# Attention and a four-expert layer on one core: the first batch runs two chunks alone, and the second batch's attention is traced inside them

## The chip, the core and the metric

The kernel runs on one core of a Trainium2 chip. TensorE (PE) multiplies matrices, VectorE (DVE), ScalarE (ACT) and GpSimd (POOL) do element-wise work, SyncE (SP) issues the DMAs. The metric is device time in microseconds (us), and lower is better. The profiled execution of the kernel before took 1321.44 us.

## The reference

Attention with a packed set of 32 queries in the middle, and then a mixture of four experts:

```python
def sm_attn(qq, kk, vv):
    s = scale * np.matmul(qq, kk.transpose(0, 1, 3, 2))
    s = s - np.max(s, axis=-1, keepdims=True)
    a = np.exp(s)
    a = a / (np.sum(a, axis=-1, keepdims=True) + 1e-09)
    return np.matmul(a, vv)
p_packed = sm_attn(p, k, v)                  # 8 batches, 8 heads, 32 packed queries, 576 keys
out = sm_attn(q, p_packed, p_packed)         # 576 tokens against the 32 packed rows
...
x = out.transpose(0, 2, 1, 3).reshape(B * S, H * D)          # 4608 x 512
p = domain_probs / (domain_probs.sum(-1, keepdims=True) + 1e-09)
for e in range(E):                           # 4 experts, 512 -> 1024 -> 512
    h = np.maximum(x @ w1[e], 0.0)
    out += p[:, e:e + 1] * (h @ w2[e])
```

All data are float32.

## The kernel before

**Units.** The expert layer is cut into 8 chunks of 512 hidden columns (`ch`, half an expert each) and the 8 batches into 4 pairs (`sb`). A unit is one chunk of one batch, and `units` lists the 64 of them in the order in which they run: chunk 0 for batch 0, chunk 0 for batch 1, chunk 1 for batch 0, and so on; after 16 units the next pair. The loop at L537 runs over them. Units are counted from 0 here.

**A unit's work.** `mm1_group` (four groups (kh, c), 12 matmuls each) multiplies the batch's token weights `xh`, `xl` (a value split into a rounded part and its rest) by `ghl`, and DVE (L310) applies relu and the probability `pbt`; the four blocks are `ablk`. `s_operand` forms with DVE (L327) the sums of a seven-product 2x2 block multiplication (`ORDER`), and splits each of the seven operands: ACT writes the rounded part (`hi_of`, L103), POOL the rest (`lo_of`, L108), both in `st`. `product` (seven per unit, 12 matmuls each) multiplies `st` by `tt`, the split block of w2, and ACT (chunk 0) or DVE (later chunks, L392) adds it to `acc`. During a unit's products the four mm1 groups of the next unit are issued between them (`GROUPS`), so PE does 84 + 48 matmuls of 288 columns per unit.

**What a unit needs beforehand.** `g_form(bs, ch, raws)` multiplies the packed attention rows `ppbd` of the batches `bs` by the w1 chunk `raws` (`wraw`) and gives `ghl`; the main loop calls it for both batches of a pair at once. `t_form(ch)` loads the w2 blocks of a chunk and makes its seven `tt` (DVE and POOL differences at L364, then the split); `tt` has 8 buffers. `t_store` writes each `tt` to `td` in DRAM while pair 0 runs, and `t_load` reads it back when a chunk comes again.

**Attention.** `pack_unit(bs, g)` (g is one half of the heads) loads k and v, multiplies p by k (`scores`), takes the softmax, transposes it (`tr`), multiplies it by v (L195) and leaves `ppbd`. `tok_unit(bs, g)` loads q, multiplies it by `ppbd`, takes the softmax over 32 rows (DVE L226, L231, L236, L242; ACT L233; DVE or POOL L232, L239) and leaves `xh`, `xl`. Both are generators, cut into steps at each `yield`; `wavefront` and `drain` run the steps. Tiles of the pool `att` (`att_tile`) have two buffers for `kt` (k or q) and `a1`, and one for `vt` (v) and `at`. For the pairs after the first, `AT_FIRST` and `AT_LATER` say at which unit a generator begins.

**The start.** Before the loop (L485 to L517) the kernel runs the attention of batches 0 and 1, `g_form` of chunk 0 for each, `t_form(0)` and the four mm1 groups of unit 0. This part is called the preparation below.

**Order.** TensorE's order within `together` is fixed by hand; the rest of each engine's order is set by a scheduler that goes through the traced program with its own estimate of times. Each engine then runs its list in order, and so does SP with the DMAs: a waiting instruction holds up everything behind it on its engine.

## Time and profile before

| | before |
|---|---|
| runs | 1322.88, 1323.24, 1323.43 us (median 1323.24) |
| profiled execution | 1321.44 us, of which the span of its instructions is 1319.6 us |
| PE / DVE / POOL / ACT busy | 1271.7 / 966.4 / 859.4 / 475.0 us |
| mean granted clock of TensorE | 0.987 of 2.4 GHz |
| DMA | 209 MB, 158 GB/s on the mean |

Times in the rows are counted from the first instruction. A row of the timeline gives its start, its length, the engine, the line of the kernel, the tile written and the tiles read (out<-in), the shapes and the number of instructions merged in it; in brackets stands how long the engine was idle before it, and who ended that wait. PE, PEld are matmuls and weight loads; a trailing q (SPq) marks the queue that issues DMAs. Matmuls overlap, so their rate is read from the distance of starts, not from their length. A matmul at L74 is recorded twice in the counts (x32 for the 16 matmuls of `scores` on both halves).

### The profile page before, as it was taken

To read this page: it belongs to the slowest core of one execution; us is meant where nothing else is said; L and a number is where in the kernel's file an instruction comes from. 1 tells how busy PE (TensorE), PEld (TensorE's weight loads), DVE (VectorE), ACT (ScalarE), POOL (GpSimd) and SP (SyncE) were. 2 spreads that over 40 slices of the span, in tenths; PEclk is the share of its full clock that TensorE was granted. 3 is DMA by queue.
4 is the path that set the end of the run, shared out by engine and by line. 5 is a ranking of instruction groups with operands and counts; after the bars stand their busy time and mean duration, and the time that the engine had idled before them with its cause. 6 is when DMAs were issued, how large, how long until landed. Compare 5 with 4: busy or idle time off the path is not lost.

```text
span 1319.6 us, 26648 instructions
## 1 busy us (share of the span) xinstructions
PE 1271.7 (96%) x10720; PEld 1178.2 (89%) x10720; DVE 966.4 (73%) x1334; ACT 475.0 (36%) x784; POOL 859.4 (65%) x578
## 2 busy tenths in 40 slices
PE   4799999899999999999999999999999999999997
PEld 2698989798899999999999998999999999999997
DVE  5767778989895676888687566699669466666668
ACT  3454434343334333333334433233323533323231
POOL 5678778798986454557568454566558655555556
PEclk8999999999999999999999999999999999999998
DMA  9536464445354545554335645443446443334422
GB/s 350 185 117 225 162 213 150 153 170 188 137 198 154 167 146 184 174 180 130 119 108 201 205 157 174 133 138 121 154 138 203 152 138 116 119 126 153 128 96 73
DMA packets 86811, 208.99 MB, mean 158 GB/s; under 512 B 8736, under 2 KB 31392, under 8 KB 86688
## 3 DMA queue, kind: packets, MB, share of 16 engines
q1 hardware_dynamic: 86016, 207.13, 46.8%
q8 instruction: 86, 1.41, 0.4%
q14 instruction: 37, 0.30, 0.1%
q10 hardware_dynamic: 672, 0.15, 0.1%
HBM read 168.37 MB, written 38.87 MB: 157 GB/s over the span
## 4 chain that ended last, share of the span: by engine, by line
PE 78%; DVE 12%; POOL 6%; DMA 2%; issue 1%; ACT 0%; POOLq 0%; SPq 0%; DVEq 0%; ACTq 0%
PE dbl L66 73%; PE dbl L74 4%; DVE sblk L327 3%; POOL st L108 3%; DVE ablk L310 1%; DVE acc L392 1%; POOL tt L108 1%; POOL acc L442 1%; PE dbl L69 1%; DVE ghl L108 1%; DVE acc L442 1%; DMA pnd<-pb 1%; DVE a L226 0%; DVE a L232 0%; DVE nb L167 0%
## 5 line engine op out<-in xcount | busy, mean ns | idle before, releaser
L66 PEld LDWEIGHTS dbl<-st,tt 128*128 128x128 f32 x5376 | 731.8, 189 | 67.7 <-POOL st L108 33.8
L66 PE MATMUL dbl<-st,tt 128*128 128x288 f32 x5376 | 774.8, 298 | 11.4 <-POOL st L108 5.2
L108 POOL TENSOR_TENSOR st<-sblk,st 128x576 fp32r<-128x576 f32 x256 | 395.4, 1551 | 215.4 <-ACT st L103 212.9
L66 PE MATMUL dbl<-xh,ghl 128*128 128x288 f32 x2048 | 418.4, 296 | 1.8 <-DVE ghl L108 1.8
L108 POOL TENSOR_TENSOR st<-ablk,st 128x576 fp32r<-128x576 f32 x192 | 286.8, 1497 | 186.5 <-ACT st L103 178.3
L392 DVE TENSOR_TENSOR acc<-dbl,acc 128x576 f32<-128x576 f32 x385 | 288.8, 752 | 118.9 <-PE dbl L66 116.5
L66 PEld LDWEIGHTS dbl<-xh,ghl 128*128 128x128 f32 x2048 | 331.0, 189 | 2.7 <-DVE ghl L108 2.7
L66 PE MATMUL dbl<-xl,ghl 128*128 128x288 f32 x1024 | 304.5, 297 | 11.5 <-POOL xl L108 5.2
L310 DVE SCALAR_TENSOR_TENSOR ablk<-dbl,pbt 128x576 f32<-128x576 f32 x256 | 192.5, 752 | 160.2 <-PE dbl L66 155.6
L103 ACT CAST st<-sblk 128x576 fp32r<-128x576 f32 x256 | 172.9, 676 | 302.2 <-DVE sblk L327 210.4
L103 ACT CAST st<-ablk 128x576 fp32r<-128x576 f32 x192 | 129.7, 676 | 227.2 <-PE dbl L66 216.3
L66 PEld LDWEIGHTS dbl<-xl,ghl 128*128 128x128 f32 x1024 | 193.6, 189 | 13.9 <-POOL xl L108 5.7
L103 ACT CAST ghl<-dbl 128x512 fp32r<-128x512 f32 x128 | 75.0, 586 | 150.9 <-PE dbl L74 89.7
L327 DVE TENSOR_TENSOR sblk<-ablk 128x576 f32<-128x576 f32 x128 | 120.3, 940 | 9.8 <-POOL acc L442 0.5
L108 DVE TENSOR_TENSOR ghl<-dbl,ghl 128x512 fp32r<-128x512 f32 x128 | 87.5, 684 | 11.3 <-ACT ghl L103 7.9
L327 DVE TENSOR_TENSOR sblk<-ablk,sblk 128x576 f32<-128x576 f32 x64 | 69.0, 1078 | 6.8 <-POOL st L108 0.9
L74 PE MATMUL dbl<-wraw,ppbd 64*32 64x512 f32 x1024 | 71.8, 602 | 0.3 <-ACT acc L390 0.3
L108 POOL TENSOR_TENSOR tt<-b,tt 128x512 fp32r<-128x512 f32 x42 | 59.5, 1427 | 4.1 <-ACT tt L103 4.0
L442 POOL TENSOR_TENSOR acc<-acc,acc 128x576 f32<-128x576 f32 x28 | 47.3, 1700 | 20.1 <-DVE acc L392 20.1
L327 DVE TENSOR_TENSOR sblk<-sblk,ablk 128x576 f32<-128x576 f32 x64 | 57.6, 899 | 1.6
L390 ACT COPY acc<-dbl 128x576 f32<-128x576 f32 x56 | 35.6, 641 | 39.7 <-PE dbl L66 39.6
L103 ACT CAST tt<-b 128x512 fp32r<-128x512 f32 x42 | 25.0, 619 | 35.5 <-DVE b L364 14.3
(63 smaller groups left out, 434.1 us busy)
## 6 DMA issues: line engine op xcount, KB each, us to landing
tt<-td SPq DMA_DIRECT2D x168, 512.0 KB, 4.3
wraw<-in_w SPq DMA_DIRECT2D x128, 256.0 KB, 3.1
td<-tt SPq DMA_DIRECT2D x56, 512.0 KB, 3.4
kt<-in_k SPq DMA_DIRECT2D x16, 576.0 KB, 6.0
kt<-in_q SPq DMA_DIRECT2D x16, 576.0 KB, 6.0
pbt<-pnd SPq DMA_DIRECT2D x32, 288.0 KB, 4.3
out<-acc SPq DMA_DIRECT2D x32, 288.0 KB, 2.4
vt<-in_v SPq DMA_DIRECT2D x16, 512.0 KB, 6.4
```

The source lines that it names most:

```text
L66: on_pe(nc.tensor.matmul(**kw))
L69: on_pe(nc.tensor.transpose(**kw))
L74: ins = nc.tensor.matmul(**kw).ins
L103: nc.scalar.copy(out=dst, in_=src)
L108: eng.tensor_tensor(out=dst, in0=src, in1=hi.bitcast(F32), op=ALU.subtract)
L310: nc.vector.scalar_tensor_tensor(out=a, in0=ps[:, :, 0:HS], scalar=0.0, in1=pbt[b][:, ts].rearrange("p (o t) -> p o t", o=1).broadcast_to( ...
L327: nc.vector.tensor_tensor(out=t, in0=blk(x), in1=blk(y), op=op)
L390: nc.scalar.copy(out=accs[b, i], in_=psv)
L392: nc.vector.tensor_tensor(out=accs[b, i], in0=psv, in1=accs[b, i], op=ALU.add)
L442: eng.tensor_tensor(out=m[dst], in0=m[x], in1=m[y], op=op)
```

## The change

`units[1]` and `units[2]` change places: batch 0 runs chunk 0 and chunk 1 (units 0 and 1), then batch 1 runs chunk 0 and chunk 1 (units 2 and 3); from unit 4 on the list is as before. The preparation holds batch 0 alone. Its q is loaded right after k and v, ahead of w1, and w1 ahead of w2. The attention of batch 1 is the generator `second`, whose steps are traced between the products of units 0 and 1 by the table `SECOND` (the 20 at unit 1 is never needed in full: `drain(second)` stands before it); its tiles all come from `att`. `g_form` for chunk 1 is called for each batch by itself, w1 of chunk 0 is loaded a second time, `t_form(1)` runs in unit 0, and `tt` of chunks 0 and 1 is read back from `td` during units 1 and 2. The attention of batches 2 and 3 begins at units 4, 7, 9 and 12 instead of 2, 5, 8 and 11.

```diff
@@ -280,6 +280,7 @@
             yield
 
     units = [(sb, ch, 2 * sb + i) for sb in range(SB) for ch in range(NCH) for i in range(2)]
+    units[1], units[2] = units[2], units[1]
     pbt = {}
 
     def load_probs(b, e):
@@ -470,51 +471,39 @@
 
     hpool = ctx.enter_context(tc.tile_pool(name="hpool", bufs=1, reuse_waits="tile"))
     with ExitStack() as first:
-        pools = [first.enter_context(tc.tile_pool(name=f"unit{u}", bufs=1)) for u in range(3)]
+        pools = [first.enter_context(tc.tile_pool(name=f"unit{u}", bufs=1)) for u in range(NG)]
 
         def unit_tile(u):
-            def new(b, shape, name):
-                if u == 3 or u == 2 and name in ("kt", "a1"):
-                    return att_tile(b, shape, name)
-                return pools[u].tile(shape, F32, name=name)
-            return new
+            return lambda b, shape, name: pools[u].tile(shape, F32, name=name)
 
         def form_tile(shape, name):
             return hpool.tile(shape, F32, name="st", bufs=4) if name == "b2" else hpool.tile(shape, F32, name="ablk", bufs=6)
 
-        packs = [pack_unit([b], g, unit_tile(2 * b + g)) for b in range(2) for g in range(NG)]
-        toks = [
-            tok_unit([b], g, unit_tile(2 * b + g), nc.gpsimd if g else nc.vector, nc.gpsimd if b else nc.scalar)
-            for b in range(2) for g in range(NG)
-        ]
+        def tok_tile(g):
+            return lambda b, shape, name: att_tile(b, shape, name) if name != "at" or g else pools[0].tile(shape, F32, name=name)
+
+        packs = [pack_unit([0], g, unit_tile(g)) for g in range(NG)]
+        toks = [tok_unit([0], g, tok_tile(g), nc.gpsimd if g else nc.vector) for g in range(NG)]
         forms = t_form(0, form_tile, {n: nc.gpsimd for n in ("t1", "t2", "t3", "t4")})
         norm_probs()
         for i in (0, 1, 0, 1):
             next(packs[i])
-        next(forms)
-        raws = w1_load(0)
-        drain(wavefront(packs[:2], 1))
         for i in range(2):
             next(toks[i])
-        for i in (2, 3, 2, 3):
-            next(packs[i])
+        raws = w1_load(0)
+        next(forms)
+        load_probs(0, 0)
+        drain(wavefront(packs, 1))
         for i in range(2):
             next(toks[i])
-        for b in range(2):
-            load_probs(b, 0)
         for _ in range(3):
             next(forms)
         drain(g_form([0], 0, raws))
-        drain(wavefront(toks[:2], 1))
+        drain(wavefront(toks, 1))
         drain(forms)
-        drain(wavefront(packs[2:], 1))
-        for i in range(2, 4):
-            next(toks[i])
         for kh, c in ((0, 0), (0, 1), (1, 1), (1, 0)):
             mm1_group(0, kh, c)
-        drain(g_form([1], 0, raws))
         raws = w1_load(1)
-        drain(wavefront(toks[2:], 1))
 
     apool = ctx.enter_context(tc.tile_pool(name="apool", bufs=2, reuse_waits="tile"))
     rpool = ctx.enter_context(tc.tile_pool(name="rpool", bufs=1, reuse_waits="tile"))
@@ -528,8 +517,14 @@
 
     nothing = iter(())
     GROUPS = {1: ((0, 0),), 3: ((0, 1),), 4: ((1, 1),), 6: ((1, 0),)}
-    GROUPS_FIRST = {4: ((0, 0), (0, 1)), 5: ((1, 1),), 6: ((1, 0),)}
-    AT_FIRST = ((2, pack_unit, 0), (5, pack_unit, 1), (8, tok_unit, 0), (11, tok_unit, 1))
+    GROUPS_LATE = {4: ((0, 0), (0, 1)), 5: ((1, 1),), 6: ((1, 0),)}
+    AT_FIRST = ((4, pack_unit, 0), (7, pack_unit, 1), (9, tok_unit, 0), (12, tok_unit, 1))
+
+    second = chain(
+        wavefront([pack_unit([1], g, att_tile) for g in range(NG)], 1),
+        wavefront([tok_unit([1], g, att_tile, nc.gpsimd if g else nc.vector) for g in range(NG)], 1),
+    )
+    SECOND = {0: (3, 3, 2, 2, 2, 2, 2), 1: (2, 2, 2, 20)}
 
     FORM_ODD, FORM_EVEN = (0, 2, 3, 5), (0, 1, 3)
     AT_LATER = ((1, pack_unit, 0), (4, pack_unit, 1), (7, tok_unit, 0), (9, tok_unit, 1))
@@ -548,9 +543,15 @@
 
         gsteps = nothing
         nsb, nch = (sb, ch + 1) if ch + 1 < NCH else (sb + 1, 0)
-        if not odd and nsb < SB:
+        if u == 0:
+            gsteps = g_form([0], 1, raws)
+        elif u == 2 or u == 3:
+            gsteps = g_form([1] if u == 2 else [0, 1], u - 1, raws)
+            drain(gsteps)
+            raws = w1_load(u)
+        elif u > 3 and not odd and nsb < SB:
             gsteps = g_form([2 * nsb, 2 * nsb + 1], nch, raws)
-        forming = odd and sb == 0 and ch + 1 < NCH
+        forming = u == 0 or u > 2 and odd and sb == 0 and ch + 1 < NCH
         if forming:
             tsteps = t_form(ch + 1, raw_tile, {"t1": nc.gpsimd, "t2": nc.vector, "t3": nc.vector, "t4": nc.gpsimd})
             next(tsteps)
@@ -562,26 +563,37 @@
             elif nxt:
                 s_operand(u + 1, n - NPROD)
             if nxt:
-                for grp in (GROUPS if u else GROUPS_FIRST).get(i, ()):
+                for grp in (GROUPS_LATE if u == 1 else GROUPS).get(i, ()):
                     mm1_group(u + 1, *grp)
-            if i in (3, 6):
+            if u == 0:
+                drain(gsteps)
+            elif i in (3, 6):
                 next(gsteps, None)
-            if i == 4 and u + 2 < len(units) and units[u + 2][1] % 2 == 0:
+            if u == 1 and i == 3:
+                drain(second)
+                drain(g_form([1], 0, raws))
+                raws = w1_load(1)
+            for _ in range(SECOND[u][i] if u in SECOND and i < len(SECOND[u]) else 0):
+                next(second, None)
+            if i == 4 and u > 1 and u + 2 < len(units) and units[u + 2][1] % 2 == 0:
                 load_probs(units[u + 2][2], units[u + 2][1] // 2)
             if i % 2 == 0:
                 next(back, None)
-            if sb == 0 and i in (FORM_ODD if odd else FORM_EVEN):
+            if sb == 0 and i in (FORM_ODD if odd or u == 0 else FORM_EVEN):
                 next(tsteps, None)
             next(sums, None)
             if sb == 0 and not odd:
                 t_store(ch, i)
-            if odd and nxt and not forming:
+            if nxt and not forming and (odd or u == 1):
                 t_load(nxt[1], i)
         drain(gsteps)
         drain(sums)
         if ch == NCH - 1 and b < B - 1:
             sums = combine(b)
-        if not odd:
+        if u == 0:
+            raws = w1_load(0)
+            load_probs(1, 0)
+        elif not odd and u > 2:
             nsb, nch = (sb, ch + 2) if ch + 2 < NCH else (sb + 1, ch + 2 - NCH)
             if nsb < SB:
                 raws = w1_load(nch)
```

The lists of the engines move as follows. Numbers tell buffers apart.

**The preparation, ACT and POOL.** ACT's list before, from the second w2 block to the first exponential of `tok_unit` (L233, on a1_331), where `tt` is being split (L103, the w2 blocks stand in ablk and st):

```order
L103 CAST tt_355<-ablk_184 128x512
L103 CAST tt_358<-ablk_182 128x512
L103 CAST tt_404<-ablk_182 128x512
L233 ACTIVATE a1_331<-a1_331 128x576
L103 CAST ghl_366<-dbl_361 128x512
```

The same place now (the exponential is that on a1_318):

```order
L188 COPY at_246<-dbl_247 128x512
L189 COPY at_246<-dbl_247 64x128
L103 CAST tt_333<-ablk_193 128x512
L103 CAST tt_338<-ablk_195 128x512
L103 CAST tt_341<-ablk_193 128x512
L233 ACTIVATE a1_318<-a1_318 128x576
L103 CAST ghl_349<-dbl_344 128x512
```

The exponential stands behind three splits of w2 blocks instead of four, and all three are of loads that now come after q and w1. POOL's list now, from the first half of the heads of batch 0 (xl_180<-at_378) to the first operands of unit 0 (st):

```order
L108 TENSOR_TENSOR xl_180<-at_378,xh_179 128x576
L239 TENSOR_TENSOR a1_330<-a1_330,s2_373 128x576
L365 TENSOR_TENSOR ablk_193<-ablk_193,st_197 128x512
L108 TENSOR_TENSOR xl_180<-at_382,xh_179 128x576
L108 TENSOR_TENSOR tt_391<-ablk_193,tt_391 128x512
L108 TENSOR_TENSOR tt_394<-st_197,tt_394 128x512
L108 TENSOR_TENSOR tt_397<-st_197,tt_397 128x512
L108 TENSOR_TENSOR tt_535<-b11_484,tt_535 128x512
L108 TENSOR_TENSOR st_476<-ablk_413,st_476 128x576
L108 TENSOR_TENSOR st_481<-sblk_479,st_481 128x576
```

Before, all seven `tt` of chunk 0 stood ahead of the first xl, and st followed the second xl at once; now four `tt` stand between the second xl and the first st.

**Unit 0, SP and PE.** SP's list now, around the load of v for the second half of the heads of batch 1 (vt_574):

```order
L219 DMA kt_805<-in_q 128x1152
L147 DMA pt_1655<-in_p 128x128
L344 DMA td1_1_101<-tt_652 128x1024
L344 DMA td1_2_102<-tt_737 128x1024
L344 DMA td1_3_103<-tt_808 128x1024
L154 DMA vt_574<-in_v 128x4x256
L158 DMA vt_574<-in_v 64x256
```

vt_574 has the one `vt` buffer of `att`, in which vt_532 (the first half) stands until PE has read it. PE's list now, at the multiplications by v:

```order
L66 MATMUL dbl_676<-xh_179,ghl_523 128x288 x2
L66 MATMUL dbl_691<-vt_532,at_632 32x64 x20
L66 MATMUL dbl_714<-vt_574,at_641 32x64 x20
L66 MATMUL dbl_741<-st_629,tt_391 128x288 x12
L66 MATMUL dbl_759<-xl_180,ghl_515 128x288
```

and before, in the preparation, where each half had a `vt` of its own:

```order
L69 MATMUL dbl_463<-ident_78,a1_447 64x128
L66 MATMUL dbl_471<-vt_316,at_453 32x64 x20
L66 MATMUL dbl_494<-vt_319,at_462 32x64 x20
L69 MATMUL dbl_517<-ident_78,ppn_492 64x128
L69 MATMUL dbl_521<-ident_78,ppn_515 64x128
```

The two multiplications by v stay neighbours, but they now stand between products, and the second reads a buffer whose load waits for the first.

**Unit 1, PE.** The list now from the scores of `tok_unit` for batch 1 (kt_803, kt_805) to the first matmuls that read its result (xl_802), at the end of unit 0 and in unit 1:

```order
L74 MATMUL dbl_847<-kt_803,ppbd1_84 32x288 x8
L74 MATMUL dbl_859<-kt_805,ppbd1_84 32x288 x8
L66 MATMUL dbl_882<-st_798,tt_535 128x288 x12
L66 MATMUL dbl_916<-st_829,tt_652 128x288 x12
L66 MATMUL dbl_951<-st_898,tt_737 128x288 x12
L66 MATMUL dbl_979<-st_932,tt_808 128x288 x12
L74 MATMUL dbl_998<-wraw_872,ppbd1_84 32x512 x2
...
L66 MATMUL dbl_1028<-st_965,tt_910 128x288 x12
L66 MATMUL dbl_1045<-xl_802,ghl_1003 128x288
```

and before, where this stood at the end of the preparation and in unit 0:

```order
L74 MATMUL dbl_615<-kt_527,ppbd1_84 32x288 x8
L74 MATMUL dbl_627<-kt_529,ppbd1_84 32x288 x8
L66 MATMUL dbl_682<-st_674,tt_350 128x288 x12
L66 MATMUL dbl_703<-st_679,tt_355 128x288 x12
L66 MATMUL dbl_724<-st_699,tt_358 128x288 x12
L66 MATMUL dbl_743<-st_720,tt_404 128x288 x12
...
L66 MATMUL dbl_779<-st_739,tt_408 128x288 x12
L66 MATMUL dbl_797<-xl_526,ghl_596 128x288
```

Between the scores and the first reader of their result stand five products and one `g_form` both times; what moved is the unit in which it happens.

## Rows read from the trace of the kernel before

**Rows 1.** The profile's page: the span, busy time of the engines with its share, TensorE's granted clock in 40 slices, and the chain of work that ended last, by engine.

```profile
span 1319.6 us, 26648 instructions
PE 1271.7 (96%) x10720; PEld 1178.2 (89%) x10720; DVE 966.4 (73%) x1334; ACT 475.0 (36%) x784; POOL 859.4 (65%) x578
...
PEclk8999999999999999999999999999999999999998
...
PE 78%; DVE 12%; POOL 6%; DMA 2%; issue 1%; ACT 0%; POOLq 0%; SPq 0%; DVEq 0%; ACTq 0%
```

**Rows 2.** Busy time by stretch: the stretch, its length, then busy us (and instructions) of PE, PEld, DVE, ACT, POOL, the granted clock, the DMA share and GB/s. The stretches end at the first mm1 of unit 0, at the first product of units 0, 1, 4 and 16, and at the end.

```profile
0.00:38.42 38.42, 19.96 (x296) 10.33 (x296) 20.73 (x51) 14.96 (x31) 20.44 (x21) 0.82 1.00 360
38.42:49.89 11.47, 10.43 (x97) 7.86 (x98) 9.22 (x14) 3.76 (x6) 6.63 (x4) 1.00 0.46 147
49.89:78.25 28.36, 22.92 (x165) 20.34 (x165) 17.21 (x27) 11.03 (x19) 17.17 (x14) 0.88 0.37 128
78.25:139.47 61.22, 59.83 (x560) 56.07 (x552) 47.14 (x59) 30.85 (x55) 54.79 (x38) 1.00 0.49 177
139.47:391.97 252.50, 239.37 (x1971) 220.85 (x1966) 213.00 (x271) 94.78 (x158) 206.60 (x140) 0.99 0.50 171
391.97:1319.60 927.63, 919.21 (x7650) 862.74 (x7648) 659.08 (x917) 319.64 (x515) 553.73 (x365) 1.00 0.45 146
```

**Rows 3.** Timeline, PE: the first product of units 60, 61 and 62.

```profile
1242.77 2.43 PE L66 MATMUL dbl<-st,tt 128*128 128x288 f32 x17
...
1262.65 1.58 PE L66 MATMUL dbl<-st,tt 128*128 128x288 f32 x10
...
1280.30 0.96 PE L66 MATMUL dbl<-st,tt 128*128 128x288 f32 x6
```

**Rows 4.** Timeline, PE, what follows the four mm1 groups of unit 0: `g_form` of chunk 0 for batch 1 (both halves), the scores of its q (both halves), and the first product of unit 0.

```profile
38.46 0.37 PE L66 MATMUL dbl<-xl,ghl 128*128 128x288 f32 x1
...
44.99 1.92 PE L74 MATMUL dbl<-wraw,ppbd 64*32 64x512 f32 x16
46.73 2.12 PE L74 MATMUL dbl<-kt,ppbd 64*32 64x288 f32 x32
49.89 6.62 PE L66 MATMUL dbl<-st,tt 128*128 128x288 f32 x48 [1.05 <-DVE ghl L108]
```

**Rows 5.** Timeline, PE: one multiplication by v with the work after it (185), and five transposes with the work after them (198), of batch 2.

```profile
185.12 0.90 PE L66 MATMUL dbl<-vt,at 128*32 128x64 f32 x40
185.95 0.40 PE L66 MATMUL dbl<-st,tt 128*128 128x288 f32 x1
...
198.54 0.71 PE L69 MATMUL dbl<-ident,a 128*128 128x128 f32 x5
199.00 1.17 PE L66 MATMUL dbl<-st,tt 128*128 128x288 f32 x7
```

**Rows 6.** The preparation: two stretches with their DMA rate (last column, GB/s); the issue of q on SP's queue; PE's wait for q; DVE's last copies into ppbd of batch 0; ACT's first split of a w2 block.

```profile
10.00:15.00 5.00, 3.30 (x90) 2.01 (x88) 1.80 (x8) 2.71 (x7) 2.04 (x2) 1.00 1.08 383
15.00:20.00 5.00, 1.62 (x16) 0.84 (x20) 0.43 (x2) 1.14 (x2) 4.19 (x4) 0.62 1.04 407
...
12.43 0.83 SPq L219 DMA_DIRECT2D kt<-in_q  x2
...
18.38 1.19 PE L74 MATMUL dbl<-kt,ppbd 64*32 64x288 f32 x8 [3.43 <-DMA kt<-in_q]
...
14.51 0.96 DVE L206 COPY ppbd<-dbl 64x64 f32<-64x64 f32 x4
...
12.18 0.62 ACT L103 CAST tt<-ablk 128x512 fp32r<-128x512 f32 x1
```

**Rows 7.** The preparation, ACT and POOL: the first exponential of `tok_unit` for batch 0; on POOL one split of tt, one difference of w2 blocks, one step of the softmax, the two xl of batch 0, and the first operand of unit 0.

```profile
24.10 0.68 ACT L233 ACTIVATE a<-a 128x576 f32<-128x576 f32 x1 [2.06 <-DVE a L232]
...
12.89 1.27 POOL L108 TENSOR_TENSOR tt<-ablk,tt 128x512 fp32r<-128x512 f32 x1 [11.59 <-ACT tt L103]
14.24 1.26 POOL L364 TENSOR_TENSOR ablk<-ablk 128x512 f32<-128x512 f32 x1
...
25.70 1.16 POOL L232 TENSOR_TENSOR a<-a,m 128x576 f32<-128x576 f32 x1 [0.56 <-DVE m L231]
...
31.00 1.39 POOL L108 TENSOR_TENSOR xl<-at,xh 128x576 fp32r<-128x576 f32 x1
...
36.21 1.40 POOL L108 TENSOR_TENSOR xl<-at,xh 128x576 fp32r<-128x576 f32 x1 [2.25 <-ACT xh L103]
41.86 1.44 POOL L108 TENSOR_TENSOR st<-ablk,st 128x576 fp32r<-128x576 f32 x1 [4.25 <-ACT st L103]
```

**Rows 8.** What the trace tells of vt: time from issue to landing of its loads over the whole run, and of the two loads issued at 122 (a stretch in which the DMA engines are 0.65 busy).

```profile
DMA to landing us min/median/max: 3.6/6.3/9.8
...
DMA to landing us min/median/max: 3.6/3.8/3.9
```

**Rows 9.** The longer waits of PE, with POOL's xl of batch 1 that ends the first of them, and the granted clock (third column from the end) in the stretches ahead of three of them and behind.

```profile
62.00 1.40 POOL L108 TENSOR_TENSOR xl<-at,xh 128x576 fp32r<-128x576 f32 x1
...
63.45 0.40 PE L66 MATMUL dbl<-xl,ghl 128*128 128x288 f32 x1 [3.76 <-POOL xl L108]
...
65.54 0.61 PE L66 MATMUL dbl<-xl,ghl 128*128 128x288 f32 x1 [1.39 <-POOL xl L108]
...
115.96 0.40 PE L66 MATMUL dbl<-xl,ghl 128*128 128x288 f32 x1 [1.39 <-DVE nb L168]
...
255.25 4.88 PE L66 MATMUL dbl<-st,tt 128*128 128x288 f32 x24 [2.72 <-DVE acc L392]
...
57.11:63.94 6.83, 3.07 (x31) 2.05 (x15) 4.59 (x7) 2.75 (x6) 6.05 (x6) 1.00 0.01 2
63.95:70.77 6.82, 5.43 (x24) 5.23 (x23) 1.45 (x2) 1.31 (x3) 3.75 (x4) 0.50 0.80 269
...
255.10:258.50 3.40, 3.25 (x13) 3.28 (x14) 2.61 (x5) 0.51 (x1) 3.09 (x3) 0.50 0.23 89
```

**Rows 10.** Timeline, PE: the first products of units 2 and 32.

```profile
95.89 0.29 PE L66 MATMUL dbl<-st,tt 128*128 128x288 f32 x1
...
704.79 1.50 PE L66 MATMUL dbl<-st,tt 128*128 128x288 f32 x10
```

## The prediction

> **What bounds the kernel now.** The page is read first: TensorE (PE) is busy 96% of the span and has 78% of the chain that ended last, DVE 12%, POOL 6% [rows 1]. Next the steady state: the first products of units 60, 61 and 62 stand 19.88 and 17.65 us apart [rows 3]. 17.65 us is a unit's 132 matmuls at full rate; 2.23 us more is `g_form` for both batches of a pair. So in steady state PE is the bound, and time can be won only where PE waits or does extra work.
>
> The table by stretch shows where that is [rows 2]. 38.42 us pass before the first mm1, with the DMA engines full (360 GB/s) and PE half idle; 11.47 us more until the first product. Units 0 to 3 take 28.36 + 61.22 = 89.58 us, and units 4 to 15 take 252.50 us. The rest, 927.63 us, is the steady state, which the change leaves alone. I cost the change up to the first product of unit 16, at 391.97 us.
>
> What is real work there? Twelve units at (17.65 + 19.88) / 2 are 225.2 us, so units 4 to 15 have 27.3 us besides: attention of batches 2 and 3, waits, and stretches at half clock. Units 0 to 3 as four units with two `g_form` are 75.1 us, so they have 14.5 us besides.
>
> **The preparation.** Before, q is issued at 12.43 and PE waits 3.43 us for it until 18.38 [rows 6]. Ahead of it stand w2 and w1, 2.1 MB; at 383 to 407 GB/s they are 5.3 us, so q now lands at about 13.1. `ppbd` is ready only at 15.5 (14.51 + 0.96), so the scores start some 2.9 us earlier.
>
> That lead does not last. w2 now comes behind 1.2 MB of q and 1.05 MB of w1: 5.7 us later. Its first block was there at 12.18 [rows 6], so now at 17.9, and the third about 2 us behind it, at 19.9. On ACT the first exponential of `tok_unit` stands behind three splits of `tt`, of which two need POOL's differences. POOL: split 1.27 from 18.6, two differences at 1.26, to 22.4 [rows 7]; ACT's two splits at 0.6 bring 23.7. The exponential was at 24.10 [rows 7]; it gains 0.4 us of the 2.9. Behind it POOL has two splits, a softmax step (1.16), a difference and another split before the first xl: 23.1 + 2 x 1.27 + 1.16 + 1.26, 0.6 for ACT, 1.27, which is 29.9; xl ends at 31.3 (before 32.4). Then softmax step, difference, xl: 35.4 by lengths alone (before 37.6). Twelve of the 48 matmuls of mm1 fit into that wait; 36 are left, at 0.136 us (48 took 6.53 us, 38.46 to 44.99 [rows 4]) 4.9 us, and 0.6 for a part at half clock: mm1 ends at about 41.0 instead of 44.99.
>
> The first product does not follow there: POOL has four `tt` (5.1 us) and then the first operand (1.44 [rows 7]) behind the second xl, which gives 42.0 and 0.3 for handing over: **42.3 instead of 49.89, 7.6 us won**. Most of it is that `g_form` and the scores of batch 1, 3.9 us with the wait of 1.05 [rows 4], are no longer here.
>
> **Units 0 to 3.** Work: four units are 70.6 us. `g_form` for one batch takes 1.74 us (44.99 to 46.73), hardly less than for two; three of these and one pair are 7.5 us, where before there were two pairs (4.5). Attention of batch 1: two scores at 2.1 [rows 4], two multiplications by v at 0.83, two transposes at 0.46 [rows 5], 0.1 for the small ones: 6.9 us. Before, half of it lay in the preparation, where PE was idle anyway. Sum 85.0 us.
>
> Waits, which the trace of before does not show as such:
>
> *The second load of v.* vt_574 cannot be issued before PE has read vt_532, and PE's next instruction needs vt_574. PE, and with it products, mm1 and all that reads them, stands for the whole load. POOL's `tt_808` must also be done, for its store stands ahead on SP's queue; by POOL's lengths that is at 55.8 (40.6 and seven operands at 1.44, a difference, three splits), while PE comes to the first v at about 57 (42.3 and four products and two mm1 groups at 1.6, `g_form` 1.74, scores 2.1, transposes 0.9), so PE's own read decides. Loads of v took 3.6 to 9.8 us, and 3.9 for the pair at 122, when the engines were 0.65 busy [rows 8]. Bounds 3.9 and 7.0; stores of three `tt` are in flight, so I take 4.5 and 0.5 for semaphore and issue: 5.0 us. The Trainium skill, "DMA: Bandwidth & Descriptors", Rules for kernel authors, speaks against such a place: issue a DMA early and wait for it late. Its Anatomy section puts a DMA at 2.0 us and bytes by 436 GB/s, an estimate of 3.2 us for 512 KB, by which the wait would be 1.3 us shorter and the sum 1.3 us less; the trace's shortest pair of 3.9 us says that is too low.
>
> *The result of `tok_unit`.* Before, its scores for batch 1 end at 48.85 and the first xl at 63.40 [rows 4, 9]: 14.5 us on DVE, ACT and POOL, behind which PE waited 1.05, 3.76 and 1.39 us. Now the same five products and one `g_form` (9.8 us) stand in between, and DVE has the accumulations of chunk 1 between its steps as well. I take 5.0 us, bounds 3 and 7. It is the same wait, one unit later, and no smaller.
>
> *Half clock.* Behind the wait of 3.76 us TensorE's granted clock was 0.50 for 6.82 us, behind that of 2.72 us for 3.40 us [rows 9]: 1.2 GHz, half of that time lost. Waits near 5 us lose 1.7 to 3.4 us each; I take 2.5 twice.
>
> *Small.* `g_form` of chunk 1 is followed at once by its reader: 0.5 us. The added DMAs (14 `tt` of 512 KB, 2 MB of w1 twice) cost nothing in the sum: units 1 to 3 moved 177 GB/s with the engines 0.49 busy [rows 2], and each load is issued when its buffer is free, five products or more ahead; without that cover each costs up to 4 us.
>
> Units 0 to 3: 85.0 + 5.0 + 5.0 + 5.0 + 0.5 = 100.5 us, where 89.58 were: **10.9 us lost**.
>
> **Units 4 to 15.** The first half of the attention of batches 2 and 3 lay in units 2 and 3. There 43.6 us (95.89 [rows 10] to 139.47) stand where 37.5 are a pair of units; 6.1 us, with the wait of 1.39 [rows 9], now fall behind unit 4. The list shows the same order two units later up to unit 8, so 252.5 becomes 258.6: **6.1 us lost**.
>
> **Sum.** -7.6 + 10.9 + 6.1 = +9.4 us on the profiled execution's 1321.44, so 1330.8. The median of the runs is 1.8 us above that execution: 1332.6, which I give as 1332 us.
>
> **The rivals.**
> *The v load is hidden* (if POOL or ACT holds PE up at that place anyway, since `at` has one buffer too and POOL is 0.65 busy): 5.0 and 2.5 us less, +1.9, 1325 us: no change that a measurement can tell, which I put at 0.2%, 2.6 us. Against it: PE's list has nothing else between the two multiplications.
> *Faster: the waits behind unit 4 shrink.* Units 2 to 15 before hold 33.4 us beyond their work at 17.65 and 2.23; some 12.6 us are attention (what a pair adds in units 16 to 31, 704.79 - 391.97 = 312.8 against 300.2 [rows 2, 10]), so about 20.8 us are waits and half clock, many of them DVE in `tok_unit` [rows 9]. `tok_unit` now begins at units 9 and 12, not 8 and 11. If this took 12 of the 20.8 us away it would decide the sign; at 15 the time is 1317 us. For it: these waits are accidents of what meets on DVE and POOL. Against: half of them belong to `pack_unit`, which moved as it was.
> *Longer waits.* The v load takes 7.0 us behind the stores, both waits cost the full 3.4 us of clock, and a late `tt` costs 4: +2.5 + 1.8 + 4, 1340 us.
>
> **How the numbers follow.** Forecast 0.52, v load hidden 0.15, fewer waits 0.17, longer waits 0.16. Slower is the first and the last, 0.68; same 0.15; faster 0.17. The forecast's own range, by the bounds of load, token wait and clock (-1.1 -2 -1.6, +2 +2 +1.8) and 2 us for the preparation, is 1325 to 1340. The range given reaches to 1318 on the fast side, which leaves most of the fast rival inside, and to 1341.
>
> **What would show it.** First product of unit 0 at 42 (40 to 45); ACT's exponential near 23.7 behind splits. In unit 0 a wait of 4 to 7 us at L195, ended by the DMA of vt; in unit 1 one of 3 to 7 us at the first mm1, ended by POOL's xl; half clock behind each. Unit 4 at about 143, unit 16 at about 401. The forecast is wrong if unit 4 begins before 137, if no DMA ends a wait in unit 0, or if units 4 to 15 take under 247 us.

## The result: 0.65% slower

The changed kernel's median is 1331.35 us (6 runs, 1329.56 to 1332.44), that of the kernel before 1323.34 us (6 runs); the ratio is 1.0065, 95% interval 1.0055 to 1.0076. The forecast was 1332 us, with 1318 to 1341 as range and 0.68 for slower.

The page of the changed kernel:

```profile
span 1329.5 us, 26677 instructions
...
PE 1274.7 (96%) x10720; PEld 1181.8 (89%) x10720; DVE 955.8 (72%) x1334; ACT 477.6 (36%) x786; POOL 859.1 (65%) x576
...
PEclk8889999999999999999999999999999999999999
...
PE 81%; DVE 11%; POOL 5%; issue 2%; DMA 2%; ACT 0%; DVEq 0%; SPq 0%; POOLq 0%; ACTq 0%
```

PE is busy for 3.0 us more than in [rows 1] with the same 10720 matmuls, and the row of the granted clock begins with three 8, where [rows 1] has one. The span is 9.9 us longer, and PE's idle time makes 6.9 of them.

The stretches of [rows 2] again, with the same cuts: at the first mm1 of unit 0, at the first product of units 0, 1, 4 and 16, and at the end:

```profile
0.00:32.50 32.50, 12.25 (x173) 6.71 (x173) 16.40 (x39) 9.69 (x19) 12.51 (x16) 0.82 0.95 321
32.50:43.68 11.18, 10.31 (x48) 9.96 (x49) 3.84 (x5) 3.56 (x7) 10.04 (x8) 0.60 0.92 363
43.68:80.84 37.16, 30.05 (x306) 24.34 (x305) 20.64 (x31) 16.77 (x32) 24.04 (x17) 0.91 0.62 207
80.84:149.01 68.17, 62.18 (x464) 56.96 (x461) 44.82 (x63) 28.63 (x48) 46.83 (x32) 0.95 0.63 219
149.01:402.44 253.43, 241.69 (x2090) 222.06 (x2089) 211.23 (x282) 99.14 (x167) 211.52 (x142) 0.99 0.52 179
402.44:1329.50 927.06, 918.24 (x7650) 861.76 (x7648) 658.91 (x917) 319.82 (x515) 554.14 (x365) 1.00 0.45 147
```

| us | forecast | measured |
|---|---|---|
| up to the first product of unit 0 | -7.6 | -6.2 (43.68 for 49.89) |
| units 0 to 3 | +10.9 | +15.7 (105.33 for 89.58) |
| units 4 to 15 | +6.1 | +0.9 (253.43 for 252.50) |
| the rest | 0 | -0.6 |

The total is right to 1 us and its terms are not: the preparation won 1.4 us less than forecast, units 0 to 3 lost 4.8 us more, units 4 to 15 lost 5.2 us less. The experiments went to these three. Against the kernel before, PE is busy for 9.5 us more in units 0 to 3 (92.23 for 82.75, work and half clock) and idle for 6.3 us more (13.10 for 6.83) [rows 2].

The waits that the forecast spoke of. In order: PE in units 0 and 1; SP's queue and POOL ahead of the load of v; POOL's xl of batch 1; the stretches of half clock behind the two waits.

```profile
59.80 0.90 PE L66 MATMUL dbl<-vt,at 128*32 128x64 f32 x40
67.52 1.45 PE L66 MATMUL dbl<-vt,at 128*32 128x64 f32 x40 [6.82 <-DMA vt<-in_v]
68.90 3.25 PE L66 MATMUL dbl<-st,tt 128*128 128x288 f32 x12
...
96.82 0.61 PE L66 MATMUL dbl<-xl,ghl 128*128 128x288 f32 x1 [5.68 <-POOL xl L108]
...
57.42 4.26 SPq L344 DMA_DIRECT2D td<-tt  x2
61.79 1.06 SPq L154 DMA_DIRECT2D vt<-in_v  x1
...
60.06 1.28 POOL L108 TENSOR_TENSOR tt<-b,tt 128x512 fp32r<-128x512 f32 x1 [1.28 <-ACT tt L103]
...
95.37 1.40 POOL L108 TENSOR_TENSOR xl<-at,xh 128x576 fp32r<-128x576 f32 x1 [2.75 <-ACT xh L103]
...
65.42:72.24 6.82, 4.72 (x54) 4.42 (x55) 0.28 (x1) 0.06 (x1) 0.99 (x1) 0.50 0.72 223
96.14:102.96 6.82, 6.14 (x25) 6.14 (x26) 1.54 (x2) 0.67 (x1) 2.03 (x2) 0.50 0.48 183
```

PE had read the first v at 60.70, but the second could not be issued before 61.79: the store of a `tt` stood ahead of it on SP's queue, and that store waited until 61.34 for POOL's split. From issue to PE's start it then took 5.73 us. Behind the wait the 12 matmuls of a product take 3.0 us (68.90 to 71.94) instead of 1.6 at 0.134 us each: the granted clock is 0.50, that is 1.2 GHz. The wait for xl is not new: the kernel before has it as well, with 3.76 and 1.39 us [rows 9].

### The profile page after: what moved, and what is told of

It reads as the page before. It is cut to its first block, busy times and chain, and to the rows that moved or that the text cites. A ratio compares the mean times of both kernels' runs of the same rounds, so it can differ in the third digit from the quotient of the medians.

```text
span 1329.5 us, 26677 instructions
## 1 busy us (share of the span) xinstructions
PE 1274.7 (96%) x10720; PEld 1181.8 (89%) x10720; DVE 955.8 (72%) x1334; ACT 477.6 (36%) x786; POOL 859.1 (65%) x576
## 4 chain that ended last, share of the span: by engine, by line
PE 81%; DVE 11%; POOL 5%; issue 2%; DMA 2%; ACT 0%; DVEq 0%; SPq 0%; POOLq 0%; ACTq 0%
PE dbl L66 76%; PE dbl L74 4%; DVE sblk L328 3%; POOL st L108 2%; DVE ablk L311 1%; POOL tt L108 1%; DVE acc L393 1%; DMA pnd<-pb 1%; DVE acc L408 1%; POOL acc L443 1%; PE dbl L69 1%; DVE ghl L108 1%; DVE acc L443 1%; DVE a L239 1%; DMA vt<-in_v 0%
## 5 line engine op out<-in xcount | busy, mean ns | idle before, releaser
L103 ACT CAST st<-sblk 128x576 fp32r<-128x576 f32 x256 | 173.1, 676 | 301.5 <-DVE sblk L328 210.9
L103 ACT CAST st<-ablk 128x576 fp32r<-128x576 f32 x192 | 129.7, 676 | 230.1 <-PE dbl L66 217.6
L103 ACT CAST ghl<-dbl 128x512 fp32r<-128x512 f32 x128 | 74.7, 587 | 146.2 <-PE dbl L74 92.3
L328 DVE TENSOR_TENSOR sblk<-ablk,sblk 128x576 f32<-128x576 f32 x64 | 65.9, 1029 | 6.8 <-DVE ablk L311 0.5
L103 ACT CAST tt<-b 128x512 fp32r<-128x512 f32 x42 | 25.2, 618 | 28.9 <-DVE b L365 11.5
```

The source lines that it names most:

```text
L103: nc.scalar.copy(out=dst, in_=src)
L328: nc.vector.tensor_tensor(out=t, in0=blk(x), in1=blk(y), op=op)
```

## The experiments

**The load of v, taken out of PE's way.** Three accumulator tiles that are idle in unit 0 take the second v of batch 1, so that nothing has to be read first.

```diff
+            if b == 1 and g == 1:        # in load_v: into spare[0..2]
+                for t, r0, rows in ((spare[0], 0, 2 * P), (spare[1], 2 * P, 2 * P), (spare[2], 4 * P, r)):
+                    ...
+                    nc.sync.dma_start(out=part[0:n], in_=v[b, r0:r0 + rows, cols_g].rearrange("(c p) d -> p c d", p=n))
+    spare = [apool.tile([P, 2, HS], F32, name=f"acc{i}") for i in (4, 5, 6)]
```

> The changed kernel (median 1331.35 us) with one load moved: v of the second half of the heads of batch 1 goes into three accumulator tiles that are idle in unit 0, so that it need not wait until PE has read the first half. Theory: the wait of 6.82 us at the second multiplication by v and the half clock behind it (6.83 us at 0.5, so 3.4 us lost) exist only because of that shared buffer. The time falls by 9 to 10 us, to 1321 to 1323 us, and no DMA ends a wait of over 1 us on PE in unit 0. Rival: PE would be held up at that place anyway, by at's single buffer or by POOL and ACT, or the wait moves on to the first mm1 of unit 1: the time falls by 3 us or less, to 1328 or more, and another wait of 4 us or more stands in unit 0 or the one of 5.68 us in unit 1 grows.

Measured: 1325.48 us, ratio to the kernel before 1.0022 (1.0012 to 1.0032); 5.9 us less by the medians, and unit 0 takes 30.77 us for 37.16. Neither number fits: the theory said 9 to 10, the rival 3 or less. The wait for a DMA is gone and two others stand in unit 0 that were not there. Unit 0, then PE at these two:

```profile
43.93:74.70 30.77, 28.29 (x307) 22.42 (x305) 18.64 (x31) 16.40 (x32) 23.67 (x17) 1.00 0.69 233
...
56.95 1.49 PE L69 MATMUL dbl<-ident,a 128*128 128x128 f32 x10 [1.49 <-ACT a L181]
...
63.21 0.65 PE L66 MATMUL dbl<-acc,at 128*32 128x64 f32 x32 [0.76 <-ACT at L198]
```

The first comes from the scheduler: a difference of w2 blocks (1.54 us on DVE), which stood ahead of the softmax, now stands between its two maxima. On ACT the split of w2 that reads it, and one more, are ahead of the exponentials, so the second of these ends at 57.53 instead of 55.78. The second is `at`, which has one buffer, as the rival held. The theory was also wrong in what the half clock costs: of its 6.82 us PE stood still for 2.1 anyway, so it lost at most (72.24 - 67.52) / 2 = 2.4 us and not 3.4. 6.8 + 2.4 - 1.5 - 0.8 is 6.9, against 6.4 by the trace; with the 2.0 us that the next kernel shows it is 6.5.

**The half clock by itself.** Matmuls that nobody reads fill both waits.

```diff
+            if b == 1 and g == 1:
+                fill(52, gs[0, 1][0])     # ahead of the second multiplication by v
...
+                if u == 1 and i == 4:
+                    fill(43, gs[1, 0][0]) # ahead of the first mm1 of unit 2
```

> The changed kernel (median 1331.35 us) with idle matmuls put into its two long waits: 52 between the two multiplications by v in unit 0 (52 times 0.134 is 7.0 us against the wait of 6.82) and 43 ahead of the first mm1 of unit 2 (5.8 us against 5.68). Their result is not read. Theory: the half clock behind each wait follows from PE standing still, and costs half of what is left of the 6.83 us when work begins again: (72.24 - 67.52) / 2 is 2.4 us and (102.97 - 96.82) / 2 is 3.1 us. The granted clock stays 1.00 in units 0 and 1, and the time falls by 4.5 to 5.5 us, to 1326 to 1327 us, though the waits themselves are as long as before. Rival: the clock falls for another reason, or the matmuls delay what the waits wait for; the time is 1330 us or more.

PE at the first wait; the stretch behind each wait; units 0 and 1; and unit 1 of the changed kernel:

```profile
59.82 7.11 PE L74 MATMUL dbl<-xh,ghl 128*128 128x288 f32 x52
66.86 0.90 PE L66 MATMUL dbl<-vt,at 128*32 128x64 f32 x40
67.69 1.87 PE L66 MATMUL dbl<-st,tt 128*128 128x288 f32 x12
...
66.80:73.60 6.80, 6.80 (x86) 6.53 (x85) 2.58 (x7) 1.79 (x4) 1.43 (x1) 1.00 0.88 260
94.20:101.00 6.80, 6.80 (x49) 6.60 (x50) 3.31 (x5) 1.35 (x2) 2.04 (x2) 1.00 0.56 205
...
43.52:78.16 34.64, 34.64 (x357) 29.39 (x357) 18.41 (x29) 16.12 (x31) 24.07 (x17) 1.00 0.69 229
78.16:106.06 27.90, 27.83 (x212) 24.18 (x208) 22.13 (x33) 8.43 (x14) 15.38 (x12) 1.00 0.74 249
...
80.84:111.16 30.32, 24.64 (x169) 21.20 (x165) 22.09 (x33) 8.43 (x14) 15.29 (x12) 0.89 0.66 231
```

Measured: 1327.88 us, ratio 1.0046 (1.0028 to 1.0064), 3.5 us less by the medians, where 4.5 to 5.5 were expected; the interval of the ratio overlaps that of the changed kernel. In the traces it is 5.25 us (1326.17 for 1331.42), but this profiled execution is the fastest of the four. There unit 0 takes 34.64 us for 37.16 and unit 1 27.90 for 30.32: 2.5 and 2.4 us, with the clock at 1.00 behind the filled waits. From the end of the wait to the end of the unit it is 11.3 us for 13.3 in unit 0 and 11.9 for 14.3 in unit 1. So the half clock comes from PE standing still, and costs 2.0 and 2.5 us, little less than the forecast put down (2.5 twice). The theory's halves, 2.4 and 3.1, are too high by about a fifth.

**The wait for tok_unit.** With v in tiles of its own, the steps of batch 1's attention are traced earlier.

```diff
-    SECOND = {0: (3, 3, 2, 2, 2, 2, 2), 1: (2, 2, 2, 20)}
+    SECOND = {0: (6, 2, 2, 4, 2, 2, 2), 1: (2, 2, 2, 20)}
```

> The kernel with v in tiles of its own (median 1325.48 us), and besides the steps of batch 1's attention taken earlier in unit 0: its scores of k behind the first product, and its scores of q with 24 products' matmuls and one mm1 group more between them and unit 1 (some 4.9 us by 3.3 for 24 matmuls and 1.6 for the group). Theory: the wait of 5.86 us at the first mm1 of unit 2 is only the length of the chain from these scores to POOL's xl, 16 us, against what stands between on PE; so 4.9 us more of cover leave a wait of 1 us or less, and no half clock behind it. The time falls by 7 to 8.5 us, to 1317 to 1318.5 us, which is faster than the kernel before. Rival: the chain is longer in unit 0, since DVE, ACT and POOL have the split of chunk 1's w2 there; the wait is 3 us or more still, or the waits of 1.5 and 0.8 us in unit 0 grow by as much; the time is 1322 us or more.

```profile
50.04 2.72 PE L66 MATMUL dbl<-st,tt 128*128 128x288 f32 x12 [2.42 <-DVE ghl L108]
...
87.30 0.40 PE L66 MATMUL dbl<-xl,ghl 128*128 128x288 f32 x1 [2.41 <-POOL xl L108]
```

Measured: 1318.45 us, ratio 0.9976 (0.9964 to 0.9987): faster than the kernel before, and by the medians 7.0 us less than without the earlier steps. The time is the theory's, the wait is not: it fell by 3.3 us (from 5.70 to 2.41) and not by 4.9 or more. From the end of the scores of q to that of xl it is now 17.8 us (69.4 to 87.2), 1.9 more, as the rival said, with operand sums of unit 1 on DVE between the steps. And the scores of k right behind `g_form` make the second product wait 2.4 us. In the profiled execution, the slowest of the 12, unit 1 takes 4.05 us less (26.20 for 30.25) and unit 4 begins 4.5 us earlier; why the medians differ by more stays open.

**The order of the first loads.** First as it was before the change (w2, w1, q), then q, w2, w1.

```diff
-        raws = w1_load(0)        # behind q
-        next(forms)
+        next(forms)              # ahead of q in the first kernel,
+        raws = w1_load(0)        # behind q in the second
```

> The changed kernel with the order of the first loads as it was before the change: w2 and w1 of the first chunk, then q. Theory of the prediction: q's lead is lost behind w2 on POOL and ACT, and POOL's chain behind the splits of w2 sets the first product, so PE's scores of q move back by about 3 us to 18, w2's first split moves forward to about 12, and the first product stays within 1.5 us of 43.68; the time is 1330 to 1333 us. Rival one: q ahead of the weights is what won the 6.2 us of the preparation; then the first product comes 3 us later, 46.5 or more, and the time is 1334 us. Rival two: q ahead does harm, since w2 comes 5.7 us later; then the first product is 2 us or more earlier and the time 1329 us or less.

The last 36 matmuls of mm1, up to the first product:

```profile
37.62:42.51 4.89, 4.89 (x37) 4.89 (x37) 2.91 (x3) 0.67 (x1) 1.43 (x1) 1.00 0.85 340
```

Measured: 1331.47 us, ratio 1.0071 (1.0055 to 1.0088): no difference to the changed kernel. PE's scores of q start at 18.41 again instead of 14.64, the first split of w2 at 12.07 instead of 18.38, the first exponential at 23.93 (24.10), and the first product at 42.51, 1.2 us earlier. So q ahead of the weights wins nothing, and the 6.2 us of the preparation belong to what was moved out of it.

> The changed kernel with w2 of the first chunk loaded ahead of w1, q still ahead of both: w2 (1.05 MB) comes about 2.6 us earlier, w1 as much later. Theory: POOL, which splits w2 and then takes the steps of tok_unit, is what the first product waits for; its first split moves from 19.08 to about 16.5, and the first product from 43.68 to 41 to 42.5; the time is 1328.5 to 1330.5 us. Rival: the chain of tok_unit from q over DVE sets it, not w2; the first product stays within 0.5 us and the time is 1331 to 1332 us.

Measured: 1337.83 us, ratio 1.0115 (1.0099 to 1.0132): 6.5 us more, where the theory said 1 to 3 less. Its first half came true: the first exponential starts at 20.77. POOL shows where the gain went; the timeline of POOL in this kernel from 31 on, and PE's first mm1 and first product:

```profile
31.43 2.48 POOL L108 TENSOR_TENSOR tt<-st,tt 128x512 fp32r<-128x512 f32 x2
33.87 1.26 POOL L108 TENSOR_TENSOR tt<-b,tt 128x512 fp32r<-128x512 f32 x1
35.09 2.77 POOL L108 TENSOR_TENSOR xl<-at,xh 128x576 fp32r<-128x576 f32 x2
...
36.54 0.61 PE L66 MATMUL dbl<-xl,ghl 128*128 128x288 f32 x1 [14.80 <-POOL xl L108]
...
45.59 0.69 PE L66 MATMUL dbl<-st,tt 128*128 128x288 f32 x4
```

Three splits of w2 that nobody waits for yet, 3.7 us, stand ahead of the two xl for which PE waits. The scheduler had put them there. The first mm1 starts at 36.54 and the first product at 45.59.

**The same loads, with POOL's order held.** The only edit to the kernel above is an order without a wait:

```diff
+            if (ch, i) in ((0, 5), (0, 6), (1, 0)):
+                after(lo.ins, last_xl[0].ins)
```

> The kernel that loads q, then w2, then w1 (median 1337.83 us), with the order of POOL alone changed: its last two splits of chunk 0's w2 and the first of chunk 1's, 3.7 us, come behind the two xl of batch 0 as in the changed kernel, and not ahead of them. Theory: w2 did come 3.3 us earlier there and the first exponential with it (20.77 against 24.10), and the gain was lost only because the scheduler put these three splits ahead of the xl. The first mm1 then starts at about 33.0 instead of 36.54 and the first product stands at 41.5 to 42.5 instead of 45.59; the time is 1333 to 1335 us, or less if the wait of 2.12 us and the half clock of unit 0 go too. Rival: w1, which comes later, is what holds mm1; the first mm1 stays behind 36.

```profile
31.09 1.40 POOL L108 TENSOR_TENSOR xl<-at,xh 128x576 fp32r<-128x576 f32 x1
32.72 1.42 POOL L108 TENSOR_TENSOR xl<-at,xh 128x576 fp32r<-128x576 f32 x1 [0.23 <-ACT xh L103]
34.09 2.52 POOL L108 TENSOR_TENSOR tt<-st,tt 128x512 fp32r<-128x512 f32 x2
...
32.54 0.61 PE L66 MATMUL dbl<-xl,ghl 128*128 128x288 f32 x1 [10.98 <-POOL xl L108]
...
40.62 1.09 PE L66 MATMUL dbl<-st,tt 128*128 128x288 f32 x7
```

Measured: 1328.04 us, ratio 1.0049 (1.0032 to 1.0066): 9.8 us less than with the scheduler's order, where 3 to 5 or more were expected. The first mm1 starts at 32.54, and the first product stands at 40.62, 5.0 us earlier and even before the expected 41.5: that much is the place of three instructions on POOL. Units 0 and 1 are 2.0 and 1.7 us shorter besides and units 4 to 15 take 1.0 us less. There the scheduler's lists of DVE, ACT and POOL changed along with the edit, so no run shows that the three instructions are the whole loss. That q, w2, w1 is a gain over the changed kernel's loads (3.3 us by the medians) is not settled by the times, for the two intervals overlap.

**The later attention of batches 2 and 3, alone.** The kernel before with one line of the change.

```diff
-    AT_FIRST = ((2, pack_unit, 0), (5, pack_unit, 1), (8, tok_unit, 0), (11, tok_unit, 1))
+    AT_FIRST = ((4, pack_unit, 0), (7, pack_unit, 1), (9, tok_unit, 0), (12, tok_unit, 1))
```

> The kernel before (median 1323.34 us) with one line of the change alone: the attention of batches 2 and 3 begins at units 4, 7, 9 and 12 and not at 2, 5, 8 and 11. The prediction held that units 2 and 3 win 6.1 us by this and units 4 to 15 lose the same 6.1 us; in the changed kernel units 4 to 15 took only 0.9 us more. Theory now: the later places meet fewer waits by themselves, so here too units 2 and 3 win about 6 us and units 4 to 15 lose only 1 us; the time is 1317 to 1320 us. Rival: the 5 us came from something else of the change (the order of the first four units, what waits they leave behind), and here the sum stays as the prediction had it: 1322.5 to 1324.5 us, with units 4 to 15 some 6 us longer than before.

Measured: 1319.48 us, ratio 0.9978 (0.9969 to 0.9987): this line is a gain by itself. Units 2 and 3 in the kernel before (its units 4 to 15 are in [rows 2]), then units 2 and 3 and units 4 to 15 with the line:

```profile
95.89:139.47 43.58, 42.19 (x422) 38.43 (x420) 35.08 (x48) 20.38 (x37) 38.43 (x27) 1.00 0.56 200
...
96.04:133.57 37.53, 37.53 (x299) 35.53 (x297) 30.59 (x36) 15.91 (x27) 36.81 (x25) 1.00 0.49 171
133.57:389.72 256.15, 243.29 (x2090) 223.26 (x2089) 212.17 (x283) 99.81 (x169) 211.95 (x142) 0.99 0.52 178
```

Units 2 and 3 win 6.05 us and units 4 to 15 lose 3.65, between the theory's 1 and the rival's 6. Of the 6.05 us only 4.66 are PE's work (42.19 - 37.53); 1.39 are the wait of [rows 9], which did not come back: PE's idle time in units 4 to 15 is 12.9 us, where it was 13.1.

**All that helped, together.** v in its own tiles, the earlier steps, q, w2, w1, and POOL's order held.

> The three edits that helped, in one kernel: v of batch 1 in tiles of its own and the steps of its attention taken earlier in unit 0 (median 1318.45 us with the changed kernel's loads), with q, w2, w1 as load order and POOL's order held (first product 40.62 instead of 43.27). Theory: the preparation and unit 0 don't share a cause, so the 2.65 us of the earlier first product add up: 1315 to 1317 us, 0.4 to 0.6% under the kernel before. Rival: an earlier first product only moves the waits, since unit 0 then meets the steps of batch 1's attention and of chunk 1's w2 where the loads are later against it; the wait of 2.57 us at the first mm1 of unit 2 grows and the time is 1318 us or more.

Measured: 1318.97 us, ratio 0.9974 (0.9962 to 0.9985); the medians do not tell it from the 1318.45 us without the last two edits. In the traces the first product is 1.9 us earlier (41.39 for 43.27) and unit 4 2.2 us (136.05 for 138.27), but the runs of either kernel spread over 5 us. Whether the 2 us are there in most runs stays open. The rival's reason is not seen: the wait at the first mm1 of unit 2 did not grow (2.42 us).

## Why the forecast was right, and where it was not

**The bound** was read rightly. The steady state has the same steps of 17.65 and 19.88 us, and everything behind unit 16 takes 927.06 us (927.63 before). The loss is all in the start. Of the signs named ahead, the first product, the exponential and both waits came where they were put; unit 4 began at 149.0 and not at 143.

**The preparation: two terms were too small, 1.4 us together.** That q's lead is lost behind w2 held fully: the first exponential is at 24.10 as before (forecast 23.7). But POOL's chain, priced "by lengths alone", was too short: the first xl ended at 32.45 and not at 31.3, the second at 36.56 and not at 35.4. (The lengths given for the second add up to 35.1, so its own sum is 0.3 us further off.) And the forecast let POOL's first operand end the preparation at 42.0 with mm1 ready at 41.0. In the trace that operand is ready at 42.90 and mm1 ends at 43.68. PE, the granted clock and POOL in the changed kernel; then the clock from 36.33 on and the first product in the kernel with the filled waits, which has the same preparation:

```profile
32.50 0.61 PE L66 MATMUL dbl<-xl,ghl 128*128 128x288 f32 x1 [13.85 <-POOL xl L108]
36.62 0.61 PE L66 MATMUL dbl<-xl,ghl 128*128 128x288 f32 x1 [0.87 <-POOL xl L108]
...
21.04:41.52 20.48, 8.15 (x32) 7.80 (x33) 8.19 (x13) 7.98 (x14) 18.59 (x16) 0.50 1.00 373
...
35.15 1.41 POOL L108 TENSOR_TENSOR xl<-at,xh 128x576 fp32r<-128x576 f32 x1 [0.36 <-ACT xh L103]
...
41.45 1.45 POOL L108 TENSOR_TENSOR st<-ablk,st 128x576 fp32r<-128x576 f32 x1
...
36.33:43.52 7.19, 5.04 (x36) 4.81 (x36) 4.79 (x6) 2.22 (x4) 7.19 (x7) 1.00 0.88 348
...
43.52 0.67 PE L66 MATMUL dbl<-st,tt 128*128 128x288 f32 x3 [1.82 <-POOL st L108]
```

PE waits 13.85 us ahead of mm1, and 9 of mm1's 11 us lie at half clock: 36 matmuls took 7.06 us where 4.9 and 0.6 were put down. That put mm1 0.78 us behind POOL's operand, and it is worth no more than that: in the kernel with the filled waits the 36 matmuls took 5.0 us at full clock, and the first product still came at 43.52, after a wait of 1.82 us for the operand (ready at 43.47 there, as one split of POOL took 1.81 us for 1.29). There POOL sets it, as the forecast had it. In the kernel before, PE had batch 1's attention from 33.46 on, and mm1 ran at full clock [rows 2]. That this work kept the clock up is not shown, for in the kernel with w2, w1, q mm1 ran at full clock from 37.62 on without it.

**Units 0 to 3: the places were right, the sizes too small by 4.8 us.** The wait for v was put at 5.0 and took 6.82. The step that failed is "PE's own read decides": SP's queue did, 1.09 us later, because POOL's split was ready at 61.34 and not at 55.8; and from issue to use the load took 5.73 us, not 5.0. Where PE's read did decide, the forecast's size was right. In three kernels SP issued the load within 0.07 us of that read, and the wait was 5.14 us (w2, w1, q), 5.01 us (q, w2, w1) and, with POOL's order held,

```profile
64.53 1.45 PE L66 MATMUL dbl<-vt,at 128*32 128x64 f32 x40 [4.78 <-DMA vt<-in_v]
```

The Trainium skill, "DMA: Bandwidth & Descriptors", Rules for kernel authors, says to issue a DMA early and to wait for it late. The trace agrees: with the load issued early, unit 0 is 6.4 us shorter. The estimate of 3.2 us from the Anatomy section of that page of the Trainium skill, which is about DMAs that GpSimd issues, is 2.5 us under the 5.73 us measured for this load of SP's.

The wait for xl took 5.68 instead of 5.0, and half clock 2.0 and 2.5 by the kernel that fills the waits (5.0 forecast). About 2.8 us are left, spread over PE's work and small waits; no run took them apart.

**Units 4 to 15: the moved work was counted with its wait.** Of the 6.1 us, 1.39 are a wait that stays away in the new place, as the kernel with the one line shows. Two more parts are seen in the trace: PE's busy time rises by 2.3 us (241.69 for 239.37) though 4.66 us of work came in, and idle time falls from 13.1 to 11.7. Most of the first is half clock, if it costs half the time that PE is busy in it: before there were two such stretches of 3.4 us, at 180.0 and 255.1, and now one, at 348.72:

```profile
348.72:352.13 3.41, 2.90 (x12) 2.93 (x13) 2.98 (x5) 0.87 (x2) 3.41 (x3) 0.50 0.11 46
```

How long it lasts may be partly luck. Behind the same wait (2.7 us, ended by DVE's accumulation) the half clock lasted 3.41 us in this kernel and in four of the others and 6.83 in four, the kernel with the one line among them; with one trace of each kernel, what decides it stays open:

```profile
333.76:340.59 6.83, 5.67 (x24) 5.70 (x25) 4.39 (x7) 2.39 (x4) 5.71 (x5) 0.50 0.38 149
```

The kernels with the changed order of units take 253.4 to 254.0 us in units 4 to 15 with the short one and 255.0 to 255.3 with the long one.

**The rivals.** "The v load is hidden" was wrong, since 6.4 us of unit 0 go when it is moved; yet its reason is there, as ACT and the one buffer of `at` bring back 2.3 us of waits once v is out of the way; POOL ends neither. "Fewer waits behind unit 4" was right in kind and came to 5.2 of the 12 us that it needed to turn the sign. With this, the errors of +4.8 and -5.2 cancelled. The range covered each of them; that the centre lies within 1 us is partly chance.

## What to carry to other kernels

When work is moved out of a start-up phase to save its time, ask what work it adds to the engine that is the bound, and what each chain of it now stands behind. Here 6 us were won ahead of the first product. Units 0 to 3 lost 15.7: TensorE was busy for 9.5 us more and idle for 6.3 us more, with one single-buffered load (a wait of 6.8 us) as the new wait. The wait for a softmax chain of 16 us with 10 us of TensorE work beside it (5.7 us) was there before as well. Issue the load into a tile that is free, and start the chain early by what the trace shows it to be long: with both, the same change was 0.24% faster than the kernel before. And compare the order of every engine after an edit to loads; a scheduler's estimate may move three instructions ahead of the one for which all wait. The kernel in which it did was 9.8 us slower than the one with that order held, 5.0 of them ahead of the first product.

## What the runs showed of the hardware

Behind waits of 2.4 us, shorter than any that the forecast had counted with, TensorE's granted clock was 0.50 for 3.4 us. The kernel before had one already (the matmul at 179.63 waited 2.41 us, half clock from 180.0); here the one behind 87.30 in the kernel with the earlier steps, and one behind a wait of 2.24 us in the kernel with all that helped:

```profile
88.19:91.60 3.41, 3.41 (x17) 3.41 (x16) 0.29 (x1) 0.57 (x1) 1.41 (x1) 0.50 1.01 400
...
47.97 0.58 PE L66 MATMUL dbl<-st,tt 128*128 128x288 f32 x1 [2.24 <-DVE ghl L108]
...
47.62:51.03 3.41, 3.06 (x13) 3.09 (x14) 2.54 (x8) 0.83 (x2) 3.41 (x3) 0.50 0.87 261
```

As an estimate, such a stretch costs half of that part of it in which TensorE has work. That is 2.4 of 6.82 us in unit 0 and 3.1 of 6.82 us in unit 1, where the filled waits gave back 2.0 and 2.5: the half is an upper bound here.
